# One 4.5 KB load moved from the scalar queue to the sync queue, between the two parts of the q weights

## The chip, the core and the metric

The kernel runs on one core of one Trainium2 chip. The metric is the device time of one execution in microseconds (us); lower is better. It is given as the median of five runs. Beside it there is one profiled execution, whose trace gives each instruction's start and duration, each DMA issue and each DMA packet. Engine names in the profile: PE is TensorE (matmul) and PEld its weight load, DVE is VectorE, ACT is ScalarE, POOL is GpSimd, SP is SyncE; a q behind the name (SPq, ACTq) is the engine's instruction queue, in which DMA issues stand. "L251" is line 251 of the kernel.

## What is computed

One decode step of a transformer layer for four sequences, one token each. Cut to what matters:

```python
# x (4,1,576); k_cache, v_cache (4,16,16384,128); wq (576,4096); wo (4096,576)
# W_gate, W_up (576,4608); W_down (4608,576); all bfloat16
def attention(x):                       # 32 query heads share 16 key/value heads
    q = (x @ wq)                        # one query per sequence and head
    k, v = last 4096 positions of k_cache, v_cache
    p = softmax(q @ k.T * 128 ** -0.5)
    return (p @ v) @ wo
def mlp(x):
    gate, up = x @ W_gate, x @ W_up
    return (relu(gate) * up) @ W_down
h   = x + attention(layernorm(x))
out = h + mlp(layernorm(h))
```

Almost all of the work is reading: the window of keys and values is 128 MB, the weights are the rest of the 159.58 MB that the profile counts as read. x itself is 4 rows of 576 bfloat16, 4.5 KB.

## The kernel before

**Order of work.** The program is written as one list per engine. `P.dma(engine, name, fn, semaphore, deps)` and the helpers `dve`, `act`, `pe` and `pool` append to the list of their engine; `emit` then writes each list in that order and puts a semaphore wait ahead of an operation whose dependencies (named by strings or tuples such as `("L", "x")`, "x is loaded") aren't known to be met. So the order in the source is the order in each queue, and an instruction that waits holds up all that stands behind it on its engine.

**Loads.** All large loads are issued on the sync queue. First the q weights, in two parts: rows 512 to 575 (L251, 512 KB, into `pT`; below: wq1), then rows 0 to 511 (L255, 4 MB, into one of four 4 MB slots of the `arena`; below: wq0). Then sixteen key tiles and sixteen value tiles of 4 MB each (L242) go round the same four slots, by the function `place`, which makes each load wait for the last reader of the bytes that it overwrites. wq0, K0, K1 and K2 need no wait; K3 waits until the q projection has read wq0, K4 until the scores of K0 are made, and so on. Behind them come the output weights (L266), gate and up (L276) and down (L284).

**The start.** x is loaded on the scalar queue (L338), behind the small activation `warm_sqrt` (L337) in program order. DVE takes its statistics (L340, L342), ACT the square root (L343), DVE normalizes (L344, L345) and copies the last 64 columns twice (L349, L350), PE transposes x and its normalized form (L361, L365), and DVE copies the result to `xnT` (L394, L396). The q projection (L382 and, by the helper, L34) needs `xnT` and wq0, and for its last fifth wq1. Its result goes through DVE and ACT (L401, L402), PE (L387) and ACT (L416) into the block form that the score matmuls use as weights.

**The rest.** Per key tile, DVE transposes it in place (L425), PE makes the scores (L449). Per four tiles a softmax follows, and PE multiplies the probabilities with the value tiles (L510). Then come the output projection, the second normalization, gate and up (L667), and down (L705), whose last pieces wait for the last loads. x is used once more there, as the residual (L693). The result's two halves leave by two stores (L712), one on the sync queue and one on the scalar queue; the sync queue waits for both at the end. L712 on the scalar queue and L338 are the only DMAs of that queue.

Of the kernel before, what the change touches and what calls it, by code (L numbers as in the profile page):

```python
# [120 lines left out]
def bass_sequential_preLN__sliding_block_cached__glu_gated_reglu__decode_kernel(  # L121
# [12 lines left out]
    with ExitStack() as es:  # L134
        cnt = [0]

        def sb(name, shape, dt):
            return es.enter_context(nc.sbuf_tensor("sb_" + name, shape, dt))

        P = Prog()  # L140
# [29 lines left out]
        x_bf = sb("x_bf", [B, D], BF16)  # L170
# [58 lines left out]
        def ring_slot():  # L229
            s = ring[0] % NSLOT  # L230
            ring[0] += 1
            return s
# [15 lines left out]
        def last_rows(W):  # L248
            return W[512:576, :].rearrange("r (a n) -> (r a) n", a=2)

        P.dma("sync", ("L", "wq", 1), lambda e: e.dma_start(out=pT[:, 0:2048], in_=last_rows(A_wq)), "d_wq1")  # L251
        s = ring_slot()
        wq_off = slot0 + s * TILE
        place(("wq", 0), wq_off, TILE, "QMM",
# [25 lines left out]
        for j in range(4):  # L280
            wd_off.append(off)
            for r0, r1 in ((0, 9),) if j < 3 else ((0, 3), (3, 6), (6, 8), (8, 9)):
                place(("wd", j, r0), off + r0 * D, (r1 - r0) * D, ("DOWN", 1),
                      lambda e, off=off, j=j, r0=r0, r1=r1: e.dma_start(  # L284
                          out=arena[:, off + r0 * D:off + r1 * D],
                          in_=B_W_down[j * 1152:(j + 1) * 1152, :].rearrange("(p r) n -> p (r n)", p=128)[:, r0 * D:r1 * D]))
# [19 lines left out]
                                                in_=c_qm[:, :, :].rearrange("p q (h j) -> p q h j", j=4),  # L306
# [4 lines left out]
                                                in_=to_v[:, :, :].rearrange("p n (k a) -> p n k a", a=4),  # L311
# [14 lines left out]
        for sg in range(2):  # L326
            pool(f"c_toq{sg + 1}", lambda e, sg=sg: e.affine_select(
                out=toq[:, :, :, :], in_=toq[:, :, :, :],
# [6 lines left out]
        dve("c_par", lambda e: e.tensor_scalar(out=par[:, 1:2], in0=par[:, 0:1], scalar1=-1.0, scalar2=1.0,  # L335
                                               op0=ALU.mult, op1=ALU.add), ["c_par0"])
        act("warm_sqrt", lambda e: e.activation(out=warm[:, 0:1], in_=eps_c[:, :], func=ACT.Sqrt), ["c_eps"])  # L337
        P.dma("scalar", ("L", "x"), lambda e: e.dma_start(out=x_bf[:, :], in_=A_x.rearrange("b s d -> (b s) d")), "d_x")  # L338
        for hf in range(2):
            dve(f"bn{hf}", lambda e, hf=hf: e.bn_stats(out=bn[:, hf, :], in_=x_bf[:, hf * 288:(hf + 1) * 288]),  # L340
                [("L", "x")] if hf == 0 else [])
# [200 lines left out]
        def finish_o():  # L542
            for q in range(4):
                for qd in range(4):
# [17 lines left out]
                                              in_=bass.AP(tensor=e8, offset=0, ap=[[8, 128], [0, 4], [1, 8]])), ["c_e8", "c_selc0"])  # L562
# [47 lines left out]
        for a in range(8):  # L610
            for n in range(2):
                for j in range(4):
# [4 lines left out]
                    else:  # L617
# [6 lines left out]
                                             in_=bass.AP(tensor=psb, offset=512 + 224, ap=[[4096, 128], [1, 64], [0, 2]])), ["part1"])  # L624
# [86 lines left out]
        for n in range(2):  # L711
            P.dma(("sync", "scalar")[n], ("O", n), lambda e, n=n: e.dma_start(  # L712
                out=orow[:, 288 * n:288 * n + 288], in_=out_sb[32 * n:32 * n + 4, :]),
# [31 lines left out]
```

## Time and profile before

| what | value |
|---|---|
| median of 5 runs | 378.27 us (377.84 to 378.5) |
| the profiled execution's own time | 377.84 us |
| its span, first to last instruction | 376.6 us |
| read from HBM | 159.58 MB, 424 GB/s over the span |
| sync queue's DMAs (q1) | 159.59 MB, 98.8% of 16 DMA engines' span |
| scalar queue's DMAs (q10) | 16 packets, 0.01 MB |
| PE, DVE, ACT, POOL busy | 56%, 60%, 14%, 3% of the span |

The span is what the profile shows; 1.24 us of the profiled execution's time lie outside it. A DMA has three moments: its issue on a queue (the DMA_DIRECT2D instruction, whose duration is only the queue's own work), the packets that the 16 DMA engines then move, and the landing, when the semaphore has its full count and waiting instructions go on. In the view of DMA activity a packet's bytes are booked where the packet starts, so that a fine slice can show more than the engines can move.

### The profile page before, as it was taken

What the parts mean: (1) busy time and instruction counts of PE and PEld (TensorE: products, weight loads), DVE (VectorE), ACT (ScalarE), POOL (GpSimd) and SP (SyncE); (2) the same over time, 40 slices, a digit from 0 to 9 for tenths busy, and PEclk for the clock granted to TensorE, in tenths of its full rate; (3) what the DMA queues carried; (4) which work ended last, traced back from release to release, by engine and by line L of the source; (5) the groups of instructions that cost most, each with busy time, mean ns of one, the idle gap of its engine ahead of it and who ended that gap; (6) DMA issues with size and microseconds to landing.
All of it is one profiled execution on the core that took longest, in us unless ns stands there. A gap on an engine that the chain in (4) does not pass through costs nothing.

```text
span 376.6 us, 2577 instructions
## 1 busy us (share of the span) xinstructions
PE 211.6 (56%) x1471; PEld 38.6 (10%) x703; DVE 227.1 (60%) x164; ACT 54.3 (14%) x85; POOL 10.5 (3%) x29
## 2 busy tenths in 40 slices
PE   0404443149919191739192845674655697777765
PEld 0000000001001010101010100110000011003322
DVE  4088878779292959593847777665659423442120
ACT  3093000301000114010101140101010401221010
POOL 8200000000000000000000000000000000000000
PEclk9965666659979687788777885968596989996689
DMA  8999999999999999999999999999999999999996
GB/s 342 439 446 435 405 439 446 432 404 446 444 435 404 439 444 439 411 432 446 439 409 432 446 439 421 420 442 435 425 428 442 426 428 428 435 423 423 435 415 255
DMA packets 6802, 159.74 MB, mean 424 GB/s; under 512 B 764, under 2 KB 904, under 8 KB 1672
## 3 DMA queue, kind: packets, MB, share of 16 engines
q1 hardware_dynamic: 6776, 159.59, 98.8%
q8 instruction: 8, 0.13, 0.1%
q14 instruction: 2, 0.02, 0.0%
q10 hardware_dynamic: 16, 0.01, 0.0%
HBM read 159.58 MB, written 0.00 MB: 424 GB/s over the span
## 4 chain that ended last, share of the span: by engine, by line
DMA 62%; DVE 18%; PE 18%; SPq 1%; issue 0%
DMA sb_arena<-in_A_k_cache_dram 53%; DVE sb_arena L425 16%; PE psb L34 11%; DMA sb_arena<-in_B_W_down_dram 9%; PE psb L449 4%; PE psb L510 3%; DVE sb_o_tmp L523 1%; DVE sb_pp L488 1%; SPq L284 1%; SPq L242 0%; PE psb L476 0%; PE psb L705 0%; DVE sb_out_sb L708 0%; SPq L255 0%; SPq L251 0%
## 5 line engine op out<-in xcount | busy, mean ns | idle before, releaser
L425 DVE STREAM_TRANSPOSE sb_arena<-sb_arena 128x8192 f32<-128x8192 f32 (+1 forms) x19 | 140.0, 7366 | 66.5 <-DMA sb_arena<-in_A_k_cache_dram 66.5
L449 PE MATMUL psb<-sb_arena 128*32 128x512 bf16 x256 | 43.0, 634 | 119.4 <-DVE sb_arena L425 119.3
L34 PE MATMUL psb<-sb_arena,sb_pp 128*128 128x512 bf16 x384 | 105.4, 384 | 0.0
L510 PE MATMUL psb<-sb_arena,sb_pp 128*128 128x512 bf16 x128 | 49.6, 388 | 8.9 <-DVE sb_o_tmp L523 8.9
L520 ACT COPY sb_o_tmp<-psb 32x512 f32<-32x512 f32 x32 | 18.5, 578 | 179.2 <-PE psb L34 178.9
L34 PE MATMUL psb<-sb_arena 128*32 128x512 bf16 x256 | 44.0, 644 | 0.0
L523 DVE TENSOR_TENSOR sb_o_tmp<-psb,sb_fm 32x512 f32<-32x512 f32 x32 | 21.7, 678 | 16.9 <-PE psb L34 16.4
L449 PEld LDWEIGHTS psb<-sb_arena 128*32 128x32 bf16 x256 | 9.6, 119 | 161.3 <-DVE sb_arena L425 132.3
L510 PEld LDWEIGHTS psb<-sb_arena,sb_pp 128*128 128x128 bf16 x128 | 12.6, 99 | 113.5 <-issue 113.5
L527 DVE TENSOR_REDUCE sb_o_sel<-sb_o_tmp 128x128 f32<-128x512 f32 x16 | 17.7, 1109 | 0.5
L468 ACT ACTIVATE sb_pp<-psb,sb_hx 128x1024 bf16<-128x1024 f32 x4 | 4.5, 1114 | 78.7 <-DVE sb_hx L465 78.7
L488 DVE TENSOR_TENSOR sb_pp<-psb,sb_m 128x1024 bf16<-128x1024 f32 x8 | 9.4, 1212 | 4.6 <-PE psb L476 4.6
L483 ACT ACTIVATE sb_pp<-psb,sb_m 128x512 bf16<-128x512 f32 x16 | 9.7, 694 | 14.8 <-PE psb L476 14.8
L526 DVE TENSOR_TENSOR sb_o_tmp<-sb_o_tmp,sb_fm 64x512 f32<-64x512 f32 x16 | 11.0, 689 | 0.5
L416 ACT COPY sb_arena<-sb_q_keep 32x256 bf16<-32x256 bf16 x8 | 9.7, 1449 | 0.1
L402 DVE CAST sb_pp<-psb 128x512 bf16<-128x512 f32 x1 | 2.4, 2428 | 10.4 <-PE psb L382 10.4
L471 DVE STREAM_TRANSPOSE sb_pp<-sb_pp 128x1024 bf16<-128x1024 bf16 x4 | 5.0, 1246 | 5.1 <-ACT sb_pp L468 5.1
L476 PE MATMUL psb<-sb_pp,sb_to_v 128*32 128x256 bf16 x64 | 4.3, 401 | 6.3 <-DVE sb_pp L471 6.3
L705 PE MATMUL psb<-sb_arena,sb_pp 128*32 128x288 bf16 x72 | 5.8, 301 | 2.5 <-DMA sb_arena<-in_B_W_down_dram 2.5
L676 DVE TENSOR_TENSOR sb_pp<-psb,sb_pp 128x384 bf16<-128x384 f32 x3 | 1.5, 552 | 9.0 <-PE psb L667 9.0
L667 PE MATMUL psb<-sb_arena,sb_hnT 128*32 128x384 bf16 x40 | 4.2, 405 | 4.0 <-DVE sb_hnT L648 2.0
L34 PE MATMUL psb<-sb_arena,sb_hnT 128*32 128x384 bf16 x80 | 6.3, 395 | 0.0
(123 smaller groups left out, 85.0 us busy)
## 6 DMA issues: line engine op xcount, KB each, us to landing
sb_arena<-in_A_k_cache_dram SPq DMA_DIRECT2D x16, 4096.0 KB, 26.2
sb_arena<-in_A_v_cache_dram SPq DMA_DIRECT2D x16, 4096.0 KB, 28.6
sb_arena<-in_A_wo_dram SPq DMA_DIRECT2D x1, 4608.0 KB, 26.2
sb_arena<-in_B_W_gate_dram SPq DMA_DIRECT2D x1, 4608.0 KB, 29.4
sb_arena<-in_A_wq_dram SPq DMA_DIRECT2D x1, 4096.0 KB, 12.6
sb_arena<-in_B_W_down_dram SPq DMA_DIRECT2D x3, 1296.0 KB, 33.5
sb_arena<-in_B_W_up_dram SPq DMA_DIRECT2D x1, 3456.0 KB, 30.4
sb_arena<-in_B_W_up_dram SPq DMA_DIRECT2D x1, 1152.0 KB, 32.8
```

Source lines behind the costliest of these rows:

```text
L34: return e.add_instruction(mybir.InstMatmult(name=e.bass.get_next_instruction_name(), engine=mybir.EngineType.PE, ins=[e.lower_ap(rhs), e. ...
L416: act("QW", lambda e, i=i, q=q: e.copy(out=bass.AP(tensor=arena, offset=32 * i * AW + 2 * i + q, ap=[[AW, 32], [512, 16], [136, 4], [32, 4]]),
L425: dve(("TRA", g), lambda e: e.transpose(out=dst, in_=src), [("L", "K", g)] if lo == 0 else [])
L449: fn = lambda e, out_=out_, lhsT=lhsT, rhs=rhs, start=start, stop=stop: e.matmul(out_, lhsT=lhsT, rhs=rhs, start=start, stop=stop, skip_gr ...
L483: act(("EV", b, 0), lambda e, a=a: e.activation(out=bass.AP(tensor=pp, offset=2 * a, ap=[[PPW, 128], [8, 2], [32, 128], [1, 2]]), in_=bank ...
L488: dve(("EV", b, 1), lambda e, n=n: e.tensor_tensor(out=bass.AP(tensor=pp, offset=16 + 8 * n, ap=[[PPW, 128], [32, 128], [2, 4], [1, 2]]), ...
L510: fn = lambda e, lhsT=lhsT, rhs=rhs, k=k, j=j: e.matmul(bank[2 + j], lhsT=lhsT, rhs=rhs, start=(k == 0), stop=(k == 7), skip_group_check=True)
L520: act(("OSC", g), lambda e, j=j: e.copy(out=o_tmp[32 * j:32 * j + 32, 0:512], in_=bank[2 + j][32 * j:32 * j + 32, :]), [("PV", g), ("OSEL" ...
L523: dve(("OSD", g), lambda e, j=j: e.tensor_tensor(out=ot(32 * j, 32), in0=bank[2 + j][32 * j:32 * j + 32, :].rearrange("p (t d) -> p t d", ...
L526: dve(("OS", g), lambda e: e.tensor_tensor(out=ot(64, 64), in0=ot(64, 64), in1=fmb(64, 64), op=ALU.mult), [("OSC", g)])
L527: dve(("OSEL", g), lambda e: e.tensor_reduce(out=o_sel[:, qd, b, :], in_=o_tmp[:, 0:512].rearrange("p (t d) -> p d t", d=DH), axis=AX.X, o ...
L705: pe(("DOWN", n), lambda e, j=j, r=r, n=n, wv=wv: e.matmul(bank[n][32 * n:32 * n + 32, 0:288], lhsT=hhT[:, r * 128 + 32 * j:r * 128 + 32 * ...
```

## The change

The load of x is taken out of the scalar queue and put into the sync queue, behind wq1 and ahead of wq0. It has the same source, the same destination and the same semaphore, and still waits for nothing.

```diff
         P.dma("sync", ("L", "wq", 1), lambda e: e.dma_start(out=pT[:, 0:2048], in_=last_rows(A_wq)), "d_wq1")
+        P.dma("sync", ("L", "x"), lambda e: e.dma_start(out=x_bf[:, :], in_=A_x.rearrange("b s d -> (b s) d")), "d_x")
         s = ring_slot()
         wq_off = slot0 + s * TILE
         place(("wq", 0), wq_off, TILE, "QMM",
...
         act("warm_sqrt", lambda e: e.activation(out=warm[:, 0:1], in_=eps_c[:, :], func=ACT.Sqrt), ["c_eps"])
-        P.dma("scalar", ("L", "x"), lambda e: e.dma_start(out=x_bf[:, :], in_=A_x.rearrange("b s d -> (b s) d")), "d_x")
         for hf in range(2):
             dve(f"bn{hf}", lambda e, hf=hf: e.bn_stats(out=bn[:, hf, :], in_=x_bf[:, hf * 288:(hf + 1) * 288]),
```

## Prediction

> **What bounds the kernel now.** I read the page's DMA lines first, then the busy time by stage, then the chain that ended last, and last the start, packet by packet.
>
> ```profile
> q1 hardware_dynamic: 6776, 159.59, 98.8%
> q10 hardware_dynamic: 16, 0.01, 0.0%
> ```
>
> The sync queue's packets fill 98.8% of what 16 DMA engines have in the span. The busy time by stage (stretch, its length, five engines' busy time, PE clock, DMA share, GB/s) shows that the missing part is at the two ends:
>
> ```profile
> 9.40:150.00 140.60, 66.42 (x466) 10.34 (x226) 100.74 (x49) 25.02 (x33) 2.67 (x4) 0.75 1.00 432
> 150.00:300.00 150.00, 89.92 (x548) 12.67 (x228) 100.30 (x61) 15.40 (x27) 0.00 (x0) 0.79 1.00 432
> ```
>
> From 9.4 to 300 us the share is 1.00 at 432 GB/s. So the end is the start of the stream, plus its bytes by that rate, plus a short tail; compute matters only where it starves the stream. The view of the key loads says how near that is:
>
> ```profile
> DMA to landing us min/median/max: 17.8/26.5/39.9
> ```
>
> A 4 MB load takes 4.19 MB / 432 GB/s = 9.7 us, yet even the latest-issued one was issued 17.8 us before it landed. So 17.8 - 9.7 = 8.1 us of lateness in compute can pass before an engine runs dry. The chain of waits begins with the issues that the change touches (start, duration):
>
> ```profile
> 0.80 0.40 SPq L251
> ...
> 1.25 0.42 SPq L255
> ...
> 1.72 0.62 SPq L242
> ```
>
> Two things are to be settled: does x put a gap into the stream at its start, and does anything get later at the end?
>
> **Step 1, the issue on the sync queue.** The change adds one DMA issue ahead of wq0 and all later loads. Its price is 0.40 us by wq1's issue, 0.56 us by x's own issue on the scalar queue; with the 0.05 us between two issues, wq0 is issued 0.45 to 0.61 us later, at 1.70 to 1.86. I take 0.61, since that row is the same transfer. Is that on the path? These are the packets from 0.5 to 3.2 us, in 40 slices of 0.0675 us:
>
> ```profile
> GB/s 0 0 0 0 0 0 0 0 0 0 0 0 0 0 0 0 0 0 0 182 303 182 546 121 303 303 121 364 17 520 442 243 486 61 728 182 607 303 425 546
> ...
> q1 hardware_dynamic: 114, 0.47, 47.4%
> q10 hardware_dynamic: 8, 0.00, 1.0%
> ```
>
> The first 19 slices are empty: wq1, issued at 0.80, has its first packet in the slice at 1.78 to 1.85 (1.83 in the packet records), 1.03 us after its issue. From 3.2 to 4.0 us, in slices of 0.02 us:
>
> ```profile
> GB/s 0 205 205 3482 2253 4916 205 410 0 1639 410 0 614 0 1639 4915 0 0 1639 1639 4915 0 0 0 0 0 0 0 0 0 0 0 0 0 0 0 0 0 0 0
> ```
>
> The slices of thousands of GB/s are the starts of wq0's 32 KB packets, one per engine, between 3.26 and 3.62 us: each engine goes from wq1 to wq0 directly. But wq0 could have started, by wq1's 1.03 us, at 1.25 + 1.03 = 2.28. It waited 0.98 us behind wq1, at the engine that was free first. With x ahead it is ready at 1.86 + 1.03 = 2.89, still 0.37 us before 3.26. The cost is **0**, and what hides it is wq1's 512 KB on the engines. Without that cover it would be 0.61 us. Even by the slowest start in the trace, x's own 2.40 - 0.94 = 1.46 us, wq0 would be ready at 3.32, a gap of 0.06 us at the first engines. Below nothing: the first issue was made while the scalar queue worked on its own at 0.94. Were that the reason why wq1 needed 1.03 us and the last store on the same queue 0.84 us, 0.19 us would be won. And 8 packets of 159 ns per engine, the plain length, are 1.27 us from 1.83, hence 3.10; the engines ended at 3.26 to 3.60, 0.16 to 0.50 later. Were all that due to x beside them, it would come back too: 0.69 us at most in all. I take nothing of it, for x has only 4 data packets of 48 to 159 ns on 4 engines.
>
> The rule that speaks against the change is in the Trainium skill, "Trainium Kernel Development and Optimization", Key Constraints: all issuing queues share the same 16 DMA engines, so a second queue saves only the sequencer's issue time. By it the move wins nothing on the engines and gives up that issue time; the sum by the rule alone would be one issue slower, and the rows above say that this time is covered.
>
> **Step 2, x's packets.** They move from q10 to q1 and stay 4 data packets and 4 of 4 B for the semaphore (q10's 16 packets are x's 8 and the store's 8). On their engines they take at most 159 + 9 ns on either queue. Difference **0**, bounded by 0.17 us either way: they cost that now, or will. A new queue boundary (wq1 to x, x to wq0) costs nothing by the stage rows: 140.6 us at 432 GB/s hold some 14 boundaries, at a share of 1.00.
>
> **Step 3, x lands later.** Now DVE's statistics start at 3.17 us without waiting, with `c_par` just done at 3.07. Behind wq1, which lands at 0.80 + 3.2 = 4.0, x lands at about 4.1: 0.9 us later. The chain from there to `xnT` takes 7.92 - 3.17 = 4.75 us, so `xnT` is ready at 8.9. The row that ends last at the q projection is another:
>
> ```profile
> 13.90 0.62 PE L382 MATMUL psb<-sb_arena,sb_xnT 128*32 128x512 bf16 x4 [6.26 <-DMA sb_arena<-in_A_wq_dram]
> ```
>
> PE waits for wq0 until 13.90; the margin left is 5.0 us. Nothing that DVE has ahead of the first key tile is pushed over its landing, since L402 follows the projection. Cost **0**. Were x to land only with wq0 (13.85), `xnT` would come at 18.6 and the q projection 4.7 us late. That is less than the 8.1 us of cover; and the first load that waits for the projection, K3, would be issued at about 23 us, with K2 still running until 43. Still 0.
>
> **Step 4, the scalar queue's first DMA.** L338 is gone from ACT, 0.56 us of queue work; ACT's next wait, for DVE's L342, then ends about 0.9 later, all before 13.9, so 0. But the store at L712 becomes the first DMA of that queue, and it ends the span. Its packets go out at 375.95 to 376.05, the sync store's at 376.05 to 376.15, so it has 0.10 us to spare. If a queue's first DMA starts more slowly, the price is 1.03 - 0.84 = 0.19 us by the sync queue's first and last, or 1.46 - (375.95 - 375.19) = 0.70 us by the scalar queue's own two (in which x may have stood behind wq1's packets). Less the spare, 0.09 to 0.60 us. A gain is excluded, because the sync store ends last now. I take 0.1, from the sync queue's rows, where nothing stood in front.
>
> **Sum.** 0 + 0 + 0 + 0.1 on the profiled execution: 377.84 + 0.1 = 377.9 us (376.6 of span, 1.24 around it). The median of the runs lies 0.43 above that execution, so the median should be **378.4 us**.
>
> **The rivals.**
>
> *The ring holds wq0 until x has landed* (slower). For it: x is a tiny transfer whose latency, issue to use, is 3.17 - 0.94 = 2.23 us, and it now stands in the one queue that must never stop. If wq0's packets start only after x's landing, they start 2.23 - 1.03 = 1.2 us later on the engines that carry x, and the load ends with its last engine: 378.27 + 1.2 = 379.5 us. Against it: the view above, where wq0's packets start in the same slices as wq1's end, while wq1 landed only at 4.0. It decides as soon as the stop exceeds the 0.37 us of cover.
>
> *Both small costs show* (slower): the gap of 0.06, the packets' 0.17 and the slow first store's 0.60 add up to 0.83 us, 379.1. Against it: each is an end of its bound.
>
> *The scalar issue disturbed the start* (faster): 0.69 back at the start and 0.17 of packets, 0.86 us, 377.4. For it: packets of up to 468 ns among wq1's. Against it: they are spread over engines without x too, as cold first reads would be.
>
> *The change does nothing at all*: x lands no later, and the store is no slower: 378.3. It falls together with the forecast.
>
> **Chances.** No change that can be told (within 0.2%, which is 0.76 us and about what a measurement of this kernel can tell): 0.60, with its own range of 377.7 to 379.0. The ring holds: 0.16. Both small costs: 0.09. Faster: 0.15. So slower 0.25, same 0.60, faster 0.15. The range takes in the ends of the bounds on both sides, 377.4 to 379.5.
>
> **What would show it.** Step 1: SP's issues L251, x, wq0 at 0.80, 1.25 and about 1.8, and wq0's first 32 KB packets still at 3.26 to 3.62. Step 2: a stage share of 1.00 from 9.4 us. Step 3: L340 at about 4.1, the transposes about 0.9 later, and the q projection still at 13.9 behind wq0. Step 4: the scalar store's packets at most 0.2 us behind the sync store's. Wrong would be: empty slices between wq1 and wq0; L382 waiting for DVE; a store that starts over 1 us after its issue; or the same start and end with another rate between them, which none of these steps would explain.

## The result, and the profile after

The changed kernel takes 379.5 us (median of 27 runs, 377.93 to 381.04) against 378.28 us for the kernel before (48 runs, 377.8 to 379.71). The ratio is 1.0031, 95% interval 1.0022 to 1.0040: slower by 0.31%, some 1.2 us. The time lies at the upper end of the predicted range (377.4 to 379.5), and the likeliest case, no change, didn't come. The runs also lie further apart: 3.1 us from lowest to highest, against 1.9 in more runs of before.

The profiled execution has a span of 377.7 us (its own time 379.02). The page's DMA queues, with x now on q1 and only the store on q10:

```profile
q1 hardware_dynamic: 6784, 159.59, 98.7%
q10 hardware_dynamic: 8, 0.00, 0.0%
```

The busy time by stage shows the stream as full as before, at 431 GB/s in place of 432:

```profile
9.40:150.00 140.60, 65.65 (x466) 10.23 (x226) 99.58 (x49) 25.02 (x33) 2.67 (x4) 0.79 1.01 431
150.00:300.00 150.00, 89.74 (x548) 12.41 (x228) 99.82 (x60) 13.91 (x25) 0.00 (x0) 0.81 1.00 431
```

So the difference is small and comes from the start. The timeline of the sync queue there (start, duration):

```profile
0.80 0.37 SPq L251 DMA_DIRECT2D sb_pp<-in_A_wq_dram  x1
1.23 0.35 SPq L252 DMA_DIRECT2D sb_x_bf<-in_A_x_dram  x1
1.63 0.34 SPq L256 DMA_DIRECT2D sb_arena<-in_A_wq_dram  x1
```

x costs the queue 0.40 us, and wq0 is issued at 1.63 where it was 1.25. The packets from 3.2 to 4.0 us in slices of 0.02 us, the view that the prediction rested on:

```profile
GB/s 2106 2048 205 410 0 205 1639 5120 205 410 205 410 0 205 0 1639 1639 3277 1639 3277 0 0 1638 0 0 0 0 0 0 0 0 0 1638 0 0 0 0 0 0 0
```

Most first packets of wq0 start by 3.66 us, in the kernel before all by 3.61. One starts in the slice at 3.84. The last one comes later still. This is the stretch from 3.9 to 4.5 us, first of the kernel before, which started no packet in it (0.00, 0), then of the changed kernel (the last two numbers are the DMA share and GB/s):

```profile
3.90:4.50 0.60, 0.00 (x0) 0.00 (x0) 0.27 (x2) 0.26 (x1) 0.60 (x1) 1.00 0.00 0
```

```profile
3.90:4.50 0.60, 0.00 (x0) 0.00 (x0) 0.60 (x2) 0.00 (x0) 0.60 (x1) 1.00 0.24 55
```

55 GB/s in 0.60 us are 33 KB: one packet of 32 KB (at 4.41 in the packet records). The two late packets took 2.17 and 2.29 us where 1.21 is the plain length. How late that makes wq0 is seen at PE, together with the moment at which x lands:

```profile
3.76 0.81 DVE L340 BATCH_NORM_STATS2 sb_bn<-sb_x_bf 4x6 f32<-4x288 bf16 x2 [0.68 <-DMA sb_x_bf<-in_A_x_dram]
...
15.57 0.62 PE L382 MATMUL psb<-sb_arena,sb_xnT 128*32 128x512 bf16 x4 [7.93 <-DMA sb_arena<-in_A_wq_dram]
```

x is 0.6 us later, far from harm; wq0 lands 1.67 us later than before (13.90). At the other end, the chain that ended last, first its last matmuls in the kernel before, then the changed kernel:

```profile
374.04 0.71 PE psb L705 x6
```

```profile
343.30 31.75 DMA sb_arena<-in_B_W_down_dram
375.04 0.04 issue
375.09 0.71 PE psb L705 x6
```

The last matmuls start at 375.09, in the kernel before at 374.04: 1.05 us of the 1.15 by which the span grew (from 376.59 to 377.74 in the traces). The stores took the rest, first the scalar queue's in the kernel before, then both in the changed one:

```profile
375.19 0.28 ACTq L712 DMA_DIRECT2D out_dram<-sb_out_sb  x1
```

```profile
376.24 0.53 ACTq L712 DMA_DIRECT2D out_dram<-sb_out_sb  x1
376.26 0.29 SPq L712 DMA_DIRECT2D out_dram<-sb_out_sb  x1
```

The scalar queue's issue is 0.53 us where it was 0.28, and from its start to the end of the span pass 1.50 us in place of 1.40.

### The profile page after: what moved, and what is told of

Same layout as the page of the kernel before. It is cut to its first block, busy times and chain, and to the rows that moved or that the text cites. A ratio compares the mean times of both kernels' runs of the same rounds, so it can differ in the third digit from the quotient of the medians.

```text
span 377.7 us, 2577 instructions
## 1 busy us (share of the span) xinstructions
PE 210.7 (56%) x1471; PEld 37.2 (10%) x703; DVE 226.3 (60%) x164; ACT 54.4 (14%) x85; POOL 10.5 (3%) x29
## 4 chain that ended last, share of the span: by engine, by line
DMA 61%; DVE 18%; PE 18%; SPq 1%; issue 0%
DMA sb_arena<-in_A_k_cache_dram 53%; DVE sb_arena L425 16%; PE psb L34 11%; DMA sb_arena<-in_B_W_down_dram 8%; PE psb L449 4%; PE psb L510 3%; DVE sb_o_tmp L523 1%; DVE sb_pp L488 1%; SPq L285 0%; SPq L242 0%; PE psb L476 0%; PE psb L705 0%; DVE sb_out_sb L708 0%; SPq L251 0%; SPq L252 0%
## 5 line engine op out<-in xcount | busy, mean ns | idle before, releaser
L449 PE MATMUL psb<-sb_arena 128*32 128x512 bf16 x256 | 42.2, 628 | 120.1 <-DVE sb_arena L425 120.1
L34 PE MATMUL psb<-sb_arena,sb_pp 128*128 128x512 bf16 x384 | 107.3, 389 | 0.0
L510 PE MATMUL psb<-sb_arena,sb_pp 128*128 128x512 bf16 x128 | 50.3, 393 | 8.9 <-DVE sb_o_tmp L523 8.9
L34 PE MATMUL psb<-sb_arena 128*32 128x512 bf16 x256 | 43.9, 648 | 0.0
L382 PE MATMUL psb<-sb_arena,sb_xnT 128*32 128x512 bf16 x16 | 2.5, 626 | 7.9 <-DMA sb_arena<-in_A_wq_dram 7.9
L34 PE MATMUL psb<-sb_arena,sb_hnT 128*32 128x384 bf16 x80 | 6.5, 406 | 0.0
```

Source lines behind the costliest of these rows:

```text
L34: return e.add_instruction(mybir.InstMatmult(name=e.bass.get_next_instruction_name(), engine=mybir.EngineType.PE, ins=[e.lower_ap(rhs), e. ...
L449: fn = lambda e, out_=out_, lhsT=lhsT, rhs=rhs, start=start, stop=stop: e.matmul(out_, lhsT=lhsT, rhs=rhs, start=start, stop=stop, skip_gr ...
L510: fn = lambda e, lhsT=lhsT, rhs=rhs, k=k, j=j: e.matmul(bank[2 + j], lhsT=lhsT, rhs=rhs, start=(k == 0), stop=(k == 7), skip_group_check=True)
```

## Experiments

The theories at first: **A**, a small DMA in the sync ring holds up the four DMA engines that carry it (the ring rival of the prediction in a milder form); **B**, wq0 is issued too late for the engines that run out of wq1 first; **C**, the scalar queue without its first DMA is to blame. Each edit is against the kernel before; the changed waits of the q projection, and the buffer and the last wait of the copy, are left out of the code shown.

### Only the issue of wq0 waits (twice)

```diff
             semk = key or "d_" + "_".join(str(v) for v in name)
+            if name == ("wq", 0):
+                deps = deps + ["c_idb"]
             P.dma("sync", ("L",) + name, make, semk, deps)
```

> x stays on the scalar queue; the issue of wq0 alone is held back, by a wait for POOL's identity (L292, done at 1.56 us before), so that it is issued at about 1.6 as in the changed kernel (1.63). Theory A, a small DMA on the sync ring holds up the four engines that carry it: no change, 378.3 us, wq0's first packets within 3.2 to 3.7. Theory B, wq0 is issued too late for the engines that are free first: late packets here as well, about 379.5. Theory C, the scalar queue without its first DMA is to blame: no change.

> The kernel in which only the issue of wq0 waits, once more. If the late issue alone carries the whole of the change's cost: 379.3 to 380.1 us, and a trace with first packets of wq0 that start up to 1 us late and take 2 us, as with x in the ring. If x in the ring adds to it: 378.3 to 379.2, with late packets of 1.5 to 1.7 us at most, as in the first trace of it.

Measured: ratio 1.0028 (1.0013 to 1.0043), and 1.0031 (1.0015 to 1.0048) the second time. That is the whole cost of the change, with x where it was. The first one's timeline:

```profile
0.80 0.41 SPq L253 DMA_DIRECT2D sb_pp<-in_A_wq_dram  x1
1.59 0.33 SPq L257 DMA_DIRECT2D sb_arena<-in_A_wq_dram  x1
...
14.41 0.62 PE L384 MATMUL psb<-sb_arena,sb_xnT 128*32 128x512 bf16 x4 [6.78 <-DMA sb_arena<-in_A_wq_dram]
```

wq0 is issued at 1.59 and lands 0.5 us later than before. This profiled execution was one of the quick ones (378.35 us, where the 12 runs reach 380.44), and so was that of the repetition, at 378.01 of 378.01 to 380.9, without a late packet:

```profile
3.90:4.50 0.60, 0.00 (x0) 0.00 (x0) 0.42 (x2) 0.11 (x1) 0.60 (x1) 1.00 0.00 0
```

What follows: issuing wq0 0.35 us later is enough, as B has it. A and C alone are out. The cost is a lottery: some executions pay nothing, others 2 us. Whether packets are as late without x in the ring as with it, the two traces don't show, as both are quick ones; the run with twice the delay, below, bears on it.

### A copy of x between wq1 and wq0, x itself as before

```diff
         P.dma("sync", ("L", "wq", 1), lambda e: e.dma_start(out=pT[:, 0:2048], in_=last_rows(A_wq)), "d_wq1")
+        P.dma("sync", ("L", "x2"), lambda e: e.dma_start(out=x_cp[:, :], in_=A_x.rearrange("b s d -> (b s) d")), "d_x2")
```

> x stays on the scalar queue and is used from there; a second copy of x, which nothing reads, is loaded on the sync queue between wq1 and wq0. Theory A: as slow as the changed kernel, about 379.5 us, with the late packets on some of four engines. Theory B: the same 379.5. Theory C: no change, 378.3.

Measured: 1.0040 (1.0023 to 1.0057). As slow as the change, though x is used from the scalar queue's load and that queue keeps its first DMA: C is out. wq0 lands later than in any trace so far:

```profile
16.19 0.62 PE L384 MATMUL psb<-sb_arena,sb_xnT 128*32 128x512 bf16 x4 [8.55 <-DMA sb_arena<-in_A_wq_dram]
```

### x behind wq0, and x ahead of wq1

```diff
               lambda e: e.dma_start(out=arena[:, wq_off:wq_off + TILE], in_=main_rows(A_wq)), key=f"slot{s}")
+        P.dma("sync", ("L", "x"), lambda e: e.dma_start(out=x_bf[:, :], in_=A_x.rearrange("b s d -> (b s) d")), "d_x")
...
-        P.dma("scalar", ("L", "x"), lambda e: e.dma_start(out=x_bf[:, :], in_=A_x.rearrange("b s d -> (b s) d")), "d_x")
```

> x on the sync queue one place later, behind wq0 and ahead of the first key tile; x then lands at about 13.9 us. Theory A: the hold-up moves to the first packets of K0, about 379.5, if it comes with every small DMA in the ring; 378.4 if it only shows where the next load's descriptors are fresh. Theory B: wq0 is issued at 1.25 again, 378.4. Theory C: 379.5.

Measured: 1.0000 (0.999 to 1.001). One place later in the queue the same transfer is free. It also tests two steps of the prediction. The statistics and the q projection in this kernel:

```profile
13.92 0.81 DVE L340 BATCH_NORM_STATS2 sb_bn<-sb_x_bf 4x6 f32<-4x288 bf16 x2 [10.85 <-DMA sb_x_bf<-in_A_x_dram]
...
17.11 0.62 PE L382 MATMUL psb<-sb_arena,sb_xnT 128*32 128x512 bf16 x4 [0.38 <-issue]
```

x lands 10.8 us later than in the kernel before, the projection starts 3.2 us later, and the time doesn't move. And the slower first issue of the store on the scalar queue (0.55 us here too) costs nothing that this interval can tell.

The other place has the same line ahead of wq1:

```diff
+        P.dma("sync", ("L", "x"), lambda e: e.dma_start(out=x_bf[:, :], in_=A_x.rearrange("b s d -> (b s) d")), "d_x")
         P.dma("sync", ("L", "wq", 1), lambda e: e.dma_start(out=pT[:, 0:2048], in_=last_rows(A_wq)), "d_wq1")
...
-        P.dma("scalar", ("L", "x"), lambda e: e.dma_start(out=x_bf[:, :], in_=A_x.rearrange("b s d -> (b s) d")), "d_x")
```

> x on the sync queue ahead of wq1. wq1 and wq0 are issued as close to one another as before, all 0.4 us later. Theory A: wq1's first packets are late on the four engines that carry x, and the rest goes on from there, 0.4 to 1.2 us more, 378.7 to 379.5. Theory B: only the later first issue counts, 378.7. Theory C: 379.5.

Measured: 1.0006 (0.9997 to 1.0016), a fifth of the change's cost. wq0 is issued as late as in the changed kernel, but wq1 is late too:

```profile
1.20 0.36 SPq L252 DMA_DIRECT2D sb_pp<-in_A_wq_dram  x1
1.62 0.42 SPq L256 DMA_DIRECT2D sb_arena<-in_A_wq_dram  x1
...
14.37 0.62 PE L382 MATMUL psb<-sb_arena,sb_xnT 128*32 128x512 bf16 x4 [6.74 <-DMA sb_arena<-in_A_wq_dram]
```

wq0 lands 0.47 us later, which is the shift of the stream by one issue (0.40) and little else. So the moment 1.6 us as such isn't the cause; the distance to the end of wq1 may be. The next runs ask that: **cover** (the time from wq0's issue to the moment at which the engines run out of work) against **moment**.

### Twice the delay

```diff
+            if name == ("wq", 0):
+                deps = deps + ["c_m41"]
```

> As the wait for the identity, but wq0 waits for POOL's L297 (done at 2.38 us before) and is issued at about 2.4; x stays on the scalar queue. Theory cover: what counts is the time from wq0's issue to the moment at which the engines run out of wq1 (3.3 to 3.6 us); it is 2.0 at least in the kernel before, 1.7 in the changed one, and would be 0.9 to 1.2 here, so more engines are late and by more: 380 to 381 us. Theory moment: an issue at 1.6 us meets something else at the start (table load, instruction fetch) and cover plays no part: 378.3 to 379.

Measured: 1.0034 (1.0022 to 1.0047), 379.11 to 379.48 in five runs. It is slower, as cover has it, but the size isn't cover's: I had expected 380 to 381. With wq0 issued at 2.40, wq0 lands late, yet hardly later than with the copy of x:

```profile
2.40 0.33 SPq L257 DMA_DIRECT2D sb_arena<-in_A_wq_dram  x1
...
16.23 0.62 PE L384 MATMUL psb<-sb_arena,sb_xnT 128*32 128x512 bf16 x4 [8.60 <-DMA sb_arena<-in_A_wq_dram]
```

In these five runs every execution paid, and about the same. The cost doesn't grow with the lost cover in proportion. And late packets come without x in the ring: by the packet records seven first packets of wq0 take 1.8 to 2.2 us here, three start only at 5.41 to 5.58, and the ends of wq0 on the engines lie 2.13 us apart (13.72 to 15.85).

### Half as much ahead of wq0, x not moved

```diff
-        P.dma("sync", ("L", "wq", 1), lambda e: e.dma_start(out=pT[:, 0:2048], in_=last_rows(A_wq)), "d_wq1")
+        P.dma("sync", ("L", "wq", 1), lambda e: e.dma_start(out=pT[:, 0:1024], in_=last_rows(A_wq)[:, 0:1024]), "d_wq1")
...
               lambda e: e.dma_start(out=arena[:, wq_off:wq_off + TILE], in_=main_rows(A_wq)), key=f"slot{s}")
+        P.dma("sync", ("L", "wq", 2), lambda e: e.dma_start(out=pT[:, 1024:2048], in_=last_rows(A_wq)[:, 1024:2048]), "d_wq2")
```

> x on the scalar queue; wq1 is cut in two by columns, the first 256 KB ahead of wq0, the other 256 KB behind it, so that wq0 is issued at 1.25 as before, with half as much ahead of it. Theory cover: the engines run out of the first half at about 2.6 to 3.0, which leaves 1.4 to 1.7 us of cover: slow like the changed kernel or slower, 379.5 to 380.5 us. Theory moment: 378.3.

Measured: 1.0028 (1.0016 to 1.0041), 378.38 to 381.0. A like cost with the issue of wq0 at 1.27 and no change to x. From 2.4 to 4.4 us, in slices of 0.05 us:

```profile
GB/s 287 374 287 205 246 205 164 778 778 1352 2007 87 655 41 41 41 2703 0 82 41 1352 656 41 41 0 41 655 0 0 0 0 0 0 0 0 0 0 655 655 0
```

wq0's first packets are strewn from 2.75 to 3.75 us. This decides between cover and moment by direction: the issue didn't move, the work ahead of it shrank, and the kernel is slower. By size it was a miss: the median of 378.81 us lies below the 379.5 to 380.5 that cover had been given. The smaller packets of the cut wq1 aren't the reason: 16 packets of 84 ns in place of 8 of 159 ns are 0.07 us more per engine.

### x in the ring, with more ahead of the next load

```diff
-        place(("wq", 0), wq_off, TILE, "QMM",
-              lambda e: e.dma_start(out=arena[:, wq_off:wq_off + TILE], in_=main_rows(A_wq)), key=f"slot{s}")
+        place(("wq", 0), wq_off, 4096, "QMM",
+              lambda e: e.dma_start(out=arena[:, wq_off:wq_off + 4096], in_=main_rows(A_wq)[:, 0:4096]), key=f"slot{s}")
+        P.dma("sync", ("L", "x"), lambda e: e.dma_start(out=x_bf[:, :], in_=A_x.rearrange("b s d -> (b s) d")), "d_x")
+        place(("wq", 2), wq_off + 4096, 12288, "QMM",
+              lambda e: e.dma_start(out=arena[:, wq_off + 4096:wq_off + TILE], in_=main_rows(A_wq)[:, 4096:16384]))
...
-        P.dma("scalar", ("L", "x"), lambda e: e.dma_start(out=x_bf[:, :], in_=A_x.rearrange("b s d -> (b s) d")), "d_x")
```

> x on the sync queue, between parts of the q weights as in the change, but with more ahead of it: wq1 (512 KB), the first quarter of wq0 (1 MB), x, the other three quarters (3 MB), K0. Theory cover: the quarter is issued at 1.25 as wq0 was before; the load behind x is issued at about 2.1 and the engines have work until about 5.8, 3.7 us later; nothing more is late than before: 378.0 to 378.5 us. Theory ring (x in the ring holds up the four engines that carry it, over and above the late issue): 378.8 to 379.5.

The changed kernel itself ran on the same chip:

> The changed kernel once more, on the chip of the two runs beside it. 379.2 to 379.8 us; in the trace, by the theory of cover, one to four engines whose first packet of wq0 starts or ends late, by 0.5 to 2 us, and the same lateness between the first and the last engine up to the end.

Measured: 1.0009 (1.0000 to 1.0018) for x behind 1.5 MB, 1.0053 (1.0039 to 1.0067) for the changed kernel beside it. x stands between two parts of the q weights in both; what differs is how long the engines have work when the next load is issued.

```profile
1.23 0.41 SPq L255 DMA_DIRECT2D sb_arena<-in_A_wq_dram  x1
1.70 0.36 SPq L256 DMA_DIRECT2D sb_x_bf<-in_A_x_dram  x1
2.10 0.34 SPq L258 DMA_DIRECT2D sb_arena<-in_A_wq_dram  x1
...
14.00 0.62 PE L384 MATMUL psb<-sb_arena,sb_xnT 128*32 128x512 bf16 x4 [3.08 <-DMA sb_arena<-in_A_wq_dram]
```

The last part of wq0 is issued at 2.10 and the projection still starts at 14.00. The changed kernel's second trace, by contrast, is the worst start of all, first the stretch from 3.9 to 4.5 us, then the projection:

```profile
3.90:4.50 0.60, 0.00 (x0) 0.00 (x0) 0.56 (x2) 0.00 (x0) 0.60 (x1) 1.00 0.66 164
```

```profile
17.33 0.62 PE L382 MATMUL psb<-sb_arena,sb_xnT 128*32 128x512 bf16 x4 [9.70 <-DMA sb_arena<-in_A_wq_dram]
```

164 GB/s are three packets there (4.11, 4.35 and 4.37; another at 4.53), of 2.1 to 2.3 us each. Three more engines begin wq0 only at 5.08, 5.10 and 5.73, by the packet records. wq0 lands 3.4 us later than in the kernel before, and the execution took 380.15 us. The median here, 380.1, is above the 379.2 to 379.8 expected.

### Versions meant to be faster

```diff
-        P.dma("sync", ("L", "wq", 1), lambda e: e.dma_start(out=pT[:, 0:2048], in_=last_rows(A_wq)), "d_wq1")
...
               lambda e: e.dma_start(out=arena[:, wq_off:wq_off + TILE], in_=main_rows(A_wq)), key=f"slot{s}")
+        P.dma("sync", ("L", "wq", 1), lambda e: e.dma_start(out=pT[:, 0:2048], in_=last_rows(A_wq)), "d_wq1")
```

> wq0 ahead of wq1, x on the scalar queue as before. Theory cover: nothing is late, 378.2 us or a little below; if the kernel before also loses something at the boundary between wq1 and wq0, this shows it, as a gain of 0.2 to 0.5. Theory moment: 378.3.

The second has the same order with x on the sync queue, between wq0 and wq1:

```diff
+        P.dma("sync", ("L", "x"), lambda e: e.dma_start(out=x_bf[:, :], in_=A_x.rearrange("b s d -> (b s) d")), "d_x")
         P.dma("sync", ("L", "wq", 1), lambda e: e.dma_start(out=pT[:, 0:2048], in_=last_rows(A_wq)), "d_wq1")
...
-        P.dma("scalar", ("L", "x"), lambda e: e.dma_start(out=x_bf[:, :], in_=A_x.rearrange("b s d -> (b s) d")), "d_x")
```

> The sync queue begins with wq0, then x, then wq1; nothing on the scalar queue at the start. Theory cover: every load behind wq0 has 10 us of cover, no engine is late, 378.2 us or a little below. Theory moment: the load issued at 1.6 us (here wq1) is late, about 379.5. x lands at about 12.5, so the q projection would start some 3 us later, which has no price by both.

The third has x on the scalar queue again and cuts wq0 as in the run with x behind 1.5 MB, with wq1 behind both parts:

```diff
-        P.dma("sync", ("L", "wq", 1), lambda e: e.dma_start(out=pT[:, 0:2048], in_=last_rows(A_wq)), "d_wq1")
...
+        place(("wq", 0), wq_off, 4096, "QMM",
...
+        place(("wq", 2), wq_off + 4096, 12288, "QMM",
...
+        P.dma("sync", ("L", "wq", 1), lambda e: e.dma_start(out=pT[:, 0:2048], in_=last_rows(A_wq)), "d_wq1")
```

> x on the scalar queue as before; the sync queue begins with the first quarter of wq0 (1 MB in rows of 8 KB), then the other three quarters, then wq1. Theory cover: the second load is issued at 1.25 and the first lasts until about 4.3 to 4.6, a cover of 3 us instead of 2.0 to 2.35, so the loss that the kernel before has in some executions is gone: 377.8 to 378.2 us. If the cover of the kernel before is already enough: 378.2. If the first reads cost more with longer rows, as with wq0 in front as a whole: 378.2 to 378.4.

Measured: 1.0011 (1.0002 to 1.0020), 1.0017 (1.0008 to 1.0026) and 1.0005 (0.9996 to 1.0014). None beats the kernel before. Whether more cover saved anything isn't shown; that the start of the stream costs more is seen in the packets of the first of them, from 1.5 to 5.5 us in slices of 0.1 us:

```profile
GB/s 0 0 0 1311 1638 328 1638 0 0 0 328 0 0 0 0 0 0 0 0 0 328 0 983 328 667 351 995 1311 328 0 0 0 0 0 655 983 328 655 983 1311
```

The first 32 KB packets start from 1.82 on (one at 2.52), the next ones only from 3.59 on: the packet records give the first ones 1.67 to 2.29 us, where a packet in the running stream takes 1.21.

## Why the prediction was right in its range and wrong in its likeliest case

**Step 1 failed**, at "with x ahead it is ready at 1.86 + 1.03 = 2.89, still 0.37 us before 3.26". The issue came a little cheaper than its bounds (wq0 is issued 0.38 us later, 0.45 to 0.61 allowed). The readiness was wrong. I took the start of the first packet after an issue, 1.03 us, as the moment from which a load can take over at full speed. But a first packet that finds its engine idle also takes longer. With wq0 at the head of the queue, issued at 0.80, the first packets take 1.67 to 2.29 us and end 2.79 to 3.57 us after the issue; less the plain 1.21 that is an estimated 1.58 to 2.36 us of cover needed, not 1.03. By direction the rows fall in line (cover: the moments at which the engines end what stands ahead, by its semaphore packets, less the issue; it is read from one or two traces per kernel):

| kernel | cover of wq0, us | ratio |
|---|---|---|
| before | 2.01 to 2.35 | 1 |
| x first | 2.18 to 2.58 | 1.0006 |
| x behind wq0 | 2.21 to 2.55 | 1.0000 |
| only the issue waits | 1.8 to 2.3 | 1.0028, 1.0031 |
| copy of x between | 1.7 to 2.0 | 1.0040 |
| changed | 1.6 to 2.2 | 1.0031, 1.0053 |
| half of wq1 ahead | 1.3 to 2.5 | 1.0028 |
| long wait | 0.9 to 1.6 | 1.0034 |
| x behind 1.5 MB | 3.7 to 4.2 | 1.0009 |

The kernel before stands at the edge: it has the cover with little to spare, and 0.38 us less falls short on some engines in some executions. Why a first packet on an idle engine takes longer, the records don't show.

The size of the loss isn't explained by this. A need of at most 2.36 us and a cover of at least 1.6 leave less than 0.8 us to lose; the changed kernel's last engine loses 1.65 us, in its second trace 3.4. In the two kernels with wq0 in front every engine has begun by 2.0 us after the issue; in the slow traces the late engines begin 2.8 us after it (4.41 less 1.63) and up to 4.1 us (5.73 less 1.66). And in the second trace eight engines that began in time have a packet of 1.5 to 2.0 us at 6.0 to 6.5. So the runs show that wq0 was issued too late against the end of the work ahead of it; what then holds single engines up for so long stays open.

**Why a late engine costs at the end** is told by the ends of loads on the first and the last of the 16 engines, from the semaphore packets (us):

| kernel | wq0 | K2 | V15 |
|---|---|---|---|
| before | 13.02 to 13.52 | 42.18 to 42.66 | 323.79 to 325.68 |
| changed | 13.20 to 15.17 | 42.67 to 44.63 | 324.53 to 326.75 |
| changed, again | 13.95 to 16.94 | 42.99 to 45.98 | 324.76 to 327.66 |
| only the issue waits, again (quick) | 13.31 to 13.65 | 42.46 to 42.78 | 324.02 to 325.87 |

An engine that is 2 or 3 us behind after wq0 is as far behind after K2: each moves its own share of a load (8 of wq0's 128 packets of 32 KB), and nothing in these traces brings it back. A load lands with its last engine. The late engine's 1.65 us (15.17 against 13.52) shrink to 1.05 at the end for a reason that the kernel before shows too: its spread grows from 0.48 to 1.89 by itself. Instruction fetches do that: the spread is 0.48 at the end of K2 and 1.57 at that of K3, and the first fetch lies between them. One 16 KB packet of the queue that the page calls "instruction" takes 0.95 us at 45.9, and the 32 KB packet behind it 1.76, so one engine loses 1.5 us; there are eight of them in the span. Part of the late start hides behind these. The other part isn't explained: the first engine, too, is 0.74 us later at V15 in the changed kernel's trace, having lost 0.5 of it by K2. A fetch can also add to a late start: in the run with the copy of x, one at 363.9 meets the engine that is last already, and the spread goes from 2.23 to 3.76 us.

**Step 2 held**: x's packets cost nothing of their own where there is cover (x behind wq0 at 1.0000, x behind 1.5 MB at 1.0009). **Step 3 held** in its result, with x later by 0.6 rather than 0.9 us; the cover that it claimed was tested with a projection 3.2 us later, at no cost. **Step 4** gave 0.1 us, and the trace has 0.10: the 1.50 us from the scalar queue's store to the end in place of 1.40. The other traces agree: 1.48 to 1.51 us in the six whose scalar queue has only the store, 1.38 to 1.40 in the eight that load x there.

**The ring rival** named 379.5 us, and that is the time measured, but not for its reason. It held that wq0 starts only after x has landed. In the changed trace most engines start wq0 before, the kernel without x in the ring is as slow, and the kernel with x behind 1.5 MB isn't slow. What it shares with the truth is its point of decision, the cover of step 1. Whether x adds something on the four engines that carry it, beyond its issue time, stays open: the three traces with x and short cover have an engine 2 to 3 us behind after wq0, the two with the wait alone 0.3 to 0.9, but these two were quick executions, the long wait has 2.1 without x in the ring, and the ratios overlap. That the measured time lies within the range is luck: the range reaches up to 379.5, the figure of this rival, whose reason didn't hold, and the step meant to give the time failed.

## What to carry to other kernels

In a kernel that is bound by one long stream of transfers, count for each issue at the start how long the engines still have work when it is made, and demand more than the time to the start of a first packet: in the table of cover, kernels with 2.0 us and more on every engine lost 0.1% or less, and those with 1.8 us or less on some lost 0.3 to 0.5%. A small transfer belongs on another queue, or behind the first loads that give cover; the same 4.5 KB were free one place later. And where the spread of the runs grows with a change, look at single engines: a mean over 16 shows a share of 1.00 while one of them is 3 us behind.

## What the runs showed of the hardware

- From a DMA issue on an idle sync queue to its first packet pass 1.03 us (kernel before), 0.63 of it after the issue instruction has ended. To the end of a first 32 KB packet pass 2.7 to 3.6 us (the two kernels with wq0 in front). The Trainium skill, "DMA: Bandwidth & Descriptors", Latency and other measured facts, has about 600 ns to the first byte for hardware-generated descriptors; counted from the end of the issue the trace's 0.63 us agrees, counted from its start 1.03 us is the figure to use here.
- Engines of one DMA didn't even out: 2.0 and 3.0 us between the first and the last after the first 4 MB load were 2.2 and 2.9 us some 310 us later (the changed kernel's two traces).
- An instruction fetch of 16 KB took one DMA engine out of the stream for about 1.5 us (0.95 us, and 1.76 in place of 1.21 for the next packet, kernel before).
- The first DMA on the scalar queue is issued more slowly (0.53 to 0.57 us against 0.27 to 0.28 for a later one), at a price of 0.10 us for the store. On the sync queue the first issue isn't slower (0.40 us, the second 0.42, kernel before).
